# The last V block of each layer in smaller pieces, with more idle products, and one load without its padding: a two-layer decode step in fp32 on one core

## The chip, the core and the metric

The kernel runs on one core of one Trainium2 chip. The metric is the device time of one execution in microseconds (us). A time is given as the median of several executions; one further execution was profiled, and every duration below comes from that one.

## The reference

One token goes through two identical layers, each an attention block over a cache of 4096 positions and a two-matrix MLP, all in fp32:

```python
def _A_ref(x, k_cache, v_cache, wq, wo):          # x 1x1x512, caches 1x32x4096x128
    q = (x @ wq).reshape(1, 1, 32, 128).transpose(0, 2, 1, 3)
    scores = einsum("bhqd,bhkd->bhqk", q, k_cache) * 128 ** -0.5
    o = einsum("bhqk,bhkd->bhqd", softmax(scores), v_cache)
    return o.transpose(0, 2, 1, 3).reshape(1, 1, 4096) @ wo     # wo 4096x512
def _B_ref(x, w1, b1, w2, b2):                     # w1 512x1376, w2 1376x512
    return gelu(x @ w1 + b1) @ w2 + b2
x = A_x
for layer in range(2):                             # the same weights and caches twice
    x = x + _A_ref(layernorm(x), k_cache, v_cache, wq, wo)
    x = x + _B_ref(layernorm(x), w1, b1, w2, b2)
```

The caches are 67 MB each, so the data that two layers read is some 288 MB.

## The kernel before, in words

**Tiling.** The 32 heads are worked in 8 groups of 4. The K of a group, and its V, is a *block*: 128 partitions by 16384 fp32, 8 MiB. A block is 8 *chunks* of 2048 columns (`NC`), 1 MiB each; chunk c holds 512 positions of each of the 4 heads. The blocks and all weights pass through one large SBUF tile, `arena`, whose regions are reused in turn. Layer 0 takes the groups from 0 to 7, layer 1 from 7 to 0. So layer 1 starts on K and V blocks that are still in SBUF, and in its second group (`n == 1`) loads only what is missing of a block.

**One group.** The scores of a chunk (`scores`, L175) are 4 products into the PSUM bank `pS`; `softmax` reduces, exponentiates and transposes them (DVE L179 to L184, ACT L186, PE L188, then the copy `pt` L190); `values` (L201) multiplies each V chunk with its part of `pt`, 4 products that accumulate in `pO`. An fp32 product shows as two MATMUL records, so a chunk is 8 records of L175 or L201. `scaled_out` (L206 to L211) takes the wanted diagonal of `pO`, and `head_out` (L229) multiplies it with the group's `wo`, summed over the groups in `pB`.

**The last group of a layer** is cut finer. Its K comes in the pieces `LAST_K`, its V in those of `LAST`, one DMA for each, and PE waits for each piece apart. The first 7 chunks go the usual way; chunk 7 is done by `scaled_out_last` (L218, 32 short matmuls into a part of `pS`), so that the long transpose of the other chunks' result runs beside it. The two small operations L221 and L223 join both, and `head_out` reads `wo`, which comes in two halves. Then follow the layer norm and `mlp`: the `w1` products (L243), gelu on DVE and ACT, and the `w2` products (L262, 11 chunks of 8 records), whose weights come in the three pieces `W2_PARTS`.

**Idle products.** `idle(t, at)` (L287) is one product of the identity with a 512-column slice of the tile `t`, whose result nobody reads. It occupies PE for two records. After the last scores of a layer `FILL` of them write `pO`; one more stands behind some of the last V chunks and writes `pS`.

**The order of DMAs.** All large loads are issued by SP, in program order (`load`, L65). Each takes the next of eight completion semaphores, and SP waits, before it issues a load, until the load eight places earlier has landed and until the engines have finished with the region that it overwrites. The order at the end of a layer is: K of the last group, `w1` (layer 0 alone), V of the last group, the two halves of `wo`, the three pieces of `w2`. The first load of layer 1 (`wq`) overwrites the first chunks of `w2` in the region `SPARE`, so it waits for the L262 products that read them.

**Padding.** On the host, each HBM row of K, V and the weights gets 1024 unused columns behind it (`PITCH`), which sets the distance between rows. One load, in layer 1's second group, takes its source without an end: `v[g][:, n_kept:]`, with `n_kept` 9216.

Of the kernel before, what the change touches and what calls it, by code (L numbers as in the profile page):

```python
# [23 lines left out]
C = 8  # L24
# [5 lines left out]
NC = 4 * U  # L30
BLOCK = 8 * NC
# [6 lines left out]
PITCH = 1024  # L38
W2_PARTS = ((0, 6), (6, 9), (9, FB))
HIDDEN = ((0, 6), (6, FB))  # L40
FILL = 2
LAST = ((0, 4), (4, 5), (5, 6), (6, 7), (7, 8))
LAST_K = ((0, 4), (4, 6), (6, 7), (7, 8))
WHOLE, HALVES = ((0, 8),), ((0, 4), (4, 8))
VAR_AT = 1
# [3 lines left out]
def decode_layers(ctx: ExitStack, tc: tile.TileContext, x, k, v, w, w1, b1, w2, b2, out):  # L49
# [8 lines left out]
    def small(name, n=1):  # L58
        return work.tile([P, n], F32, name=name, bufs=2 if name in ("xs", "x_sum", "rstd", "sc", "nsc") else 1)
# [3 lines left out]
    def load(at, src):  # L63
        t = arena[:, at : at + src.shape[-1]]
        tc.keep_in_program_order(nc.sync.dma_start(t, src))  # L65
        return t
# [65 lines left out]
    def mean_of(xs, s, at):  # L132
        nm = minus_mean(s, at)
        xc, sq, ss = small("xc", 4), small("sq", 4), small("ss")
        nc.vector.tensor_scalar(xc, xs[:, :, 0], nm, None, op0=ALU.add)
        nc.vector.scalar_tensor_tensor(sq, xc, 1.0, xc, op0=ALU.mult, op1=ALU.mult, accum_out=ss)
        return nm, ss, xc

    def rstd_of(ss, at):
        nv = minus_mean(ss, at)  # L140
        ve, r = small("ve"), small("rstd")
        tc.keep_in_program_order(
            nc.vector.tensor_scalar(ve, nv, -1.0, EPS, op0=ALU.mult, op1=ALU.add))
        nc.gpsimd.tensor_tensor(r, ve, power, op=ALU.pow)
        return r

    def query_block(c, xs, wt):
        for j in range(J):
            nc.tensor.matmul(pQ[32 * j : 32 * j + 2, :], xs[:, c, :],  # L149
                             wt[:, c, :].rearrange("p (h j q) -> p j h q", h=4, j=J)[:, j],  # L150
                             start=(c == 0), stop=(c == 3))

    def first_queries(nm):
        qt = work.tile([P, P], F32, name="wide")
        nc.vector.transpose(qt, pQ)
        z = zq[0]
        nc.vector.scalar_tensor_tensor(z[:, :, C - 1], of_32(qt, J, 1), nm, of_32(qt, J),
                                       op0=ALU.mult, op1=ALU.add)
        return z
# [13 lines left out]
    def scores(z, c, kt):  # L173
        for j in range(J):
            nc.tensor.matmul(pS[32 * j : 32 * j + C, :], z[:, j, C - 1 - c : 2 * C - 1 - c],  # L175
                             kt[:, j, :], start=(c == 0), stop=(c == C - 1))
# [22 lines left out]
    def values(i, pt, vt, c, of=C):  # L199
        for j in range(J):  # L200
            nc.tensor.matmul(pO[32 * j : 32 * j + 4, :], pt[:, j, c, :], vt[:, j, :],  # L201
                             start=(i == 0), stop=(i == of - 1))
# [72 lines left out]
    def stream(what, g, pieces, base):  # L275

        for a, b in pieces:
            t = load(base + NC * a, part(k if what == "k" else v, g, a, b))
            for c in range(a, b):
                here[what, g, c] = chunk(t, c - a)  # L280
                yield c, here[what, g, c]
# [4 lines left out]
    def idle(t, at):  # L286
        tc.keep_in_program_order(nc.tensor.matmul(at[:C, :], ident[:, :C], t[:, 0, :], start=True, stop=True))  # L287

    for layer in range(2):
        order = list(range(G)) if layer == 0 else list(range(G))[::-1]  # L290
        for c in range(4):
            query_block(c, xs, wq_first)
            if c == 1:
                nm, ss, xc = mean_of(xs, s, pB[:, P : P + 1])
        negm, xc_l = small("negm"), small("xc_l", 4)
        nc.vector.tensor_copy(negm, nm)
        z = first_queries(negm)
        r = rstd_of(ss, pB[:, P + 1 : P + 2])
        nc.vector.tensor_copy(xc_l, xc)
        sc, nsc = small("sc"), small("nsc")  # L300
        nc.vector.tensor_scalar(sc, r, DH ** -0.5, None, op0=ALU.mult)
        nc.vector.tensor_scalar(nsc, r, -(DH ** -0.5), None, op0=ALU.mult)
        for n, g in enumerate(order):
            first, final = n == 0, n == G - 1

            k_home, v_home = ((2 * n + i) % 3 * BLOCK for i in (1, 2))
            if layer == 1:
                k_home, v_home = 12 * NC if n == 2 else BLOCK, 0

            if layer == 1 and n == 0:  # L310
                tiles = [(c, here["k", g, c]) for c in range(C)]
            elif layer == 1 and n == 1:
                tiles = [(c, here["k", g, c]) for c in range(2)]
                tiles += list(stream("k", g, ((2, 3), (3, 4), (4, 8)), -2 * NC))
            else:
                halves = first or (layer == 1 and n == 2)
                tiles = stream("k", g, LAST_K if final else HALVES if halves else WHOLE, k_home)
            for c, t in tiles:
                scores(z, c, t)
            if final:  # L320
                for _ in range(FILL):
                    idle(t, pO)
            pt, rl = softmax(sc, nsc)
            if layer == 1 and n == 0:
                z = queries(n + 1, xc_l, wq_next, pH, False)

            if layer == 1 and n == 0:
                for c in range(C):
                    values(c, pt, here["v", g, c], c)
            elif layer == 1 and n == 1:  # L330
                at, n_kept = 6 * NC, STAY + U * KEPT
                load(at + n_kept - 3 * NC, v[g][:, n_kept:])
                nc.scalar.copy(arena[:, at : at + STAY - 3 * NC], arena[:, SPARE - STAY + 3 * NC : SPARE])
                for i in range(KEPT):
                    to = at + STAY - 3 * NC + U * i
                    nc.scalar.copy(arena[:, to : to + U], pK[i])
                for c in range(C):
                    values(c, pt, here["v", g, c] if c < 3 else chunk(arena[:, at:], c - 3), c)
            elif final:
                if layer == 0:  # L340
                    load(HELD, w1)
                for c, t in stream("v", g, LAST, v_home):
                    if c < C - 1:
                        values(c, pt, t, c, C - 1)
                    if c == C - 2:
                        others = scaled_out(rl)
                    if 3 <= c < C - 1:
                        idle(t, pS)
            else:
                for c, t in stream("v", g, WHOLE, v_home):  # L350
                    for i in range(KEPT):
                        if layer == 0 and n == G - 2 and c == (STAY + U * i) // NC:
                            nc.scalar.copy(pK[i], t[:, STAY // U % J + i - J * (c - STAY // NC), :])
                    values(c, pt, t, c)

            if layer == 1 and n == 0:
                wo_t = chunk(arena[:, PAIR : PAIR + NC])
            elif final:
                last_v = t
                at = PAIR + NC * layer  # L360
                for i in range(2):
                    load(at + NC // 2 * i, of_w(wo_at(g), 1)[:, NC // 2 * i : NC // 2 * (i + 1)])
                wo_t = chunk(arena[:, at : at + NC])
                for a, b in W2_PARTS:
                    load(SPARE + U * a, w2[:, U * a : U * b])
            else:
                t = load(PAIR, of_w(wo_at(g) if layer == 0 else wq_at(g - 1), 2))
                wo_t, wq_next = (chunk(t, i) for i in ((0, 1) if layer == 0 else (1, 0)))
            on = scaled_out_last(rl, pt, last_v, others) if final else scaled_out(rl)
            head_out(on, wo_t, first, final)  # L370
            if not final and not (layer == 1 and n == 0):
                z = queries(n + 1, xc_l, wq_next, pO, layer == 0 and n == G - 2)
        at = work.tile([P, P], F32, name="wide")
        nc.vector.transpose(at, pW)
        x1, s1 = set_x(of_32(at, 4), 1.0, xs[:, :, 0])
        mt, xb = mlp(x1, s1, w1_t, w2_t)
        if layer == 0:
            xs, s = set_x(of_32(mt, 4), 0.5, xb)
            g = G - 2
            wq_first = wq_next  # L380
            wq_next = chunk(load(SPARE, of_w(wq_at(g), 1)))
            for c in range(2):
                here["k", g, c] = chunk(load(SPARE + NC * (c + 1), part(k, g, c, c + 1)))
# [43 lines left out]
```

## Time and profile before

| | |
|---|---|
| median of 3 executions | 685.1 us (684.95 to 686.89) |
| the profiled execution, its own time | 685.56 us |
| its span, first to last instruction | 683.8 us |
| mean granted TensorE clock | 0.748 |
| PE matmul busy | 362.6 us (53%) |
| VectorE busy | 111.8 us (16%) |
| ScalarE busy | 21.6 us (3%) |
| HBM read | 287.52 MB, 420 GB/s over the span |

The times of instructions and DMAs are counted from the start of the span. "PEclk" is the clock that TensorE was granted, 1.00 being full speed. The DMA share is the mean busy share of the core's 16 DMA engines; it can read a little over 1 in a short window.

### The profile page before, as it was taken

To read this page: it belongs to the slowest core of one execution; us is meant where nothing else is said; L and a number is where in the kernel's file an instruction comes from. 1 tells how busy PE (TensorE), PEld (TensorE's weight loads), DVE (VectorE), ACT (ScalarE), POOL (GpSimd) and SP (SyncE) were. 2 spreads that over 40 slices of the span, in tenths; PEclk is the share of its full clock that TensorE was granted. 3 is DMA by queue.
4 is the path that set the end of the run, shared out by engine and by line. 5 is a ranking of instruction groups with operands and counts; after the bars stand their busy time and mean duration, and the time that the engine had idled before them with its cause. 6 is when DMAs were issued, how large, how long until landed. Compare 5 with 4: busy or idle time off the path is not lost.

```text
span 683.8 us, 7178 instructions
## 1 busy us (share of the span) xinstructions
PE 362.6 (53%) x3240; PEld 106.2 (16%) x3240; DVE 111.8 (16%) x376; ACT 21.6 (3%) x48; POOL 3.5 (1%) x17
## 2 busy tenths in 40 slices
PE   2533563456534555246657886462345534655767
PEld 0001120011111111102114222110011111211213
DVE  1002120121201212012105122120121201202013
ACT  0000000000000000001000200000000000000000
POOL 0000000000000000000000000000000000000000
PEclk9967776766656777677769998676777757666889
DMA  9999999999999999999997999999999999999995
GB/s 369 430 433 453 453 427 429 426 430 427 429 427 422 450 441 434 429 406 428 440 407 320 442 425 452 437 427 429 429 430 427 434 430 414 453 434 414 428 411 217
DMA packets 11550, 287.97 MB, mean 421 GB/s; under 512 B 1792, under 2 KB 1792, under 8 KB 2816
## 3 DMA queue, kind: packets, MB, share of 16 engines
q1 hardware_dynamic: 11088, 287.51, 98.0%
q8 instruction: 25, 0.41, 0.2%
q10 hardware_dynamic: 432, 0.01, 0.0%
q14 instruction: 5, 0.04, 0.0%
HBM read 287.52 MB, written 0.00 MB: 420 GB/s over the span
## 4 chain that ended last, share of the span: by engine, by line
DMA 41%; PE 36%; another core or an unknown queue 16%; DVE 4%; ACT 1%; issue 1%; SPq 0%; ACTq 0%; DVEq 0%
DMA arena<-in_v 40%; PE pO L201 20%; PE pS L175 10%; PE pB L229 2%; ACT wide L186 1%; PE pS L287 1%; PE pO L168 1%; PE pO L188 1%; PE pO L262 1%; DMA xcol<-in_x 1%; DVE mx L179 1%; DVE wide L206 1%; PE pS L243 0%; PE pO L149 0%
## 5 line engine op out<-in xcount | busy, mean ns | idle before, releaser
L175 PE MATMUL pS<-arena,zq 128*8 128x512 f32 x1024 | 148.4, 730 | 136.5 <-DMA arena<-in_k 136.2
L201 PE MATMUL pO<-arena,pt 128*4 128x512 f32 x1008 | 148.0, 727 | 108.6 <-DMA arena<-in_v 108.2
L175 PEld LDWEIGHTS pS<-arena,zq 128*8 128x8 f32 x1024 | 29.7, 103 | 243.3 <-DMA arena<-in_k 137.5
L201 PEld LDWEIGHTS pO<-arena,pt 128*4 128x4 f32 x1008 | 28.8, 98 | 212.7 <-issue 211.4
L179 DVE TENSOR_REDUCE mx<-pS 128x1 f32<-128x512 f32 x16 | 11.1, 692 | 292.7 <-PE pS L175 292.7
L188 PE MATMUL pO<-ident,wide 128*128 128x128 f32 x64 | 12.3, 323 | 41.4 <-ACT wide L186 41.4
L186 ACT ACTIVATE wide<-pS,bias,sc 128x512 f32<-128x512 f32 x16 | 12.4, 777 | 548.8 <-DVE bias L184 548.8
L166 DVE SCALAR_TENSOR_TENSOR arena<-arena,xc_l 128x512 f32<-128x512 f32 x39 | 29.3, 752 | 1.4
L164 DVE TENSOR_SCALAR arena<-arena,xc_l 128x512 f32<-128x512 f32 x13 | 6.3, 486 | 130.9 <-DMA arena<-in_w 130.3
L206 DVE STREAM_TRANSPOSE wide<-pO 128x512 f32<-128x512 f32 x16 | 11.5, 717 | 89.7 <-PE pO L201 89.7
L229 PE MATMUL pB<-arena,on 128*1 128x128 f32 x448 | 18.6, 315 | 7.0 <-DVE on L211 7.0
L168 PE MATMUL pO<-one,arena 128*128 128x1 f32 x96 | 12.9, 256 | 11.0 <-DVE wide L206 9.3
L188 PEld LDWEIGHTS pO<-ident,wide 128*128 128x128 f32 x64 | 7.9, 159 | 55.4 <-ACT wide L186 50.4
L168 PEld LDWEIGHTS pO<-one,arena 128*128 128x128 f32 x96 | 11.9, 195 | 21.5 <-DVE wide L206 19.6
L229 PEld LDWEIGHTS pB<-arena,on 128*1 128x1 f32 x448 | 11.6, 93 | 12.1 <-DVE on L211 10.3
L287 PE MATMUL pS<-arena,ident 128*8 128x512 f32 x16 | 8.2, 592 | 0.0
L192 DVE STREAM_TRANSPOSE mt<-ls 128x32 f32<-128x32 f32 x16 | 3.4, 212 | 17.5 <-ACT wide L186 17.5
L262 PE MATMUL pO<-arena,gelu_g 128*1 128x128 f32 x176 | 5.2, 272 | 1.8 <-DVE gelu_g L258 1.8
L262 PEld LDWEIGHTS pO<-arena,gelu_g 128*1 128x1 f32 x176 | 4.3, 84 | 2.8 <-DVE gelu_g L258 2.5
L190 DVE COPY pt<-pO 128x128 f32<-128x128 f32 x16 | 4.2, 261 | 1.2 <-PE pO L188 1.2
L170 DVE COPY zq<-pO 128x4 f32<-128x4 f32 x13 | 2.1, 165 | 12.9 <-PE pO L168 12.9
L236 POOL TENSOR_TENSOR xb<-xs,b2c 128x4 f32<-128x4 f32 x2 | 0.4, 201 | 654.9 <-DVE xs L123 654.9
(94 smaller groups left out, 99.3 us busy)
## 6 DMA issues: line engine op xcount, KB each, us to landing
arena<-in_k SPq DMA_DIRECT2D x7, 4096.0 KB, 23.6
arena<-in_w SPq DMA_DIRECT2D x13, 2048.0 KB, 35.8
arena<-in_v SPq DMA_DIRECT2D x3, 4096.0 KB, 28.7
arena<-in_k SPq DMA_DIRECT2D x8, 1024.0 KB, 21.8
arena<-in_v SPq DMA_DIRECT2D x8, 1024.0 KB, 32.8
arena<-in_k SPq DMA_DIRECT2D x2, 2048.0 KB, 41.8
arena<-in_w SPq DMA_DIRECT2D x6, 512.0 KB, 25.2
arena<-in_w SPq DMA_DIRECT2D x2, 1536.0 KB, 25.9
```

Of the source, the lines that this page charges most:

```text
L164: nc.vector.tensor_scalar(t, wt[:, 0, :], xc[:, 0:1], None, op0=ALU.mult)
L166: nc.vector.scalar_tensor_tensor(t, wt[:, c, :], xc[:, c : c + 1], t, op0=ALU.mult, op1=ALU.add)
L168: nc.tensor.matmul(at[:, j : j + 1], t[:, P * j : P * (j + 1)], one, start=True, stop=True)
L175: nc.tensor.matmul(pS[32 * j : 32 * j + C, :], z[:, j, C - 1 - c : 2 * C - 1 - c], kt[:, j, :], start=(c == 0), stop=(c == C - 1))
L179: nc.vector.tensor_reduce(mx[:, 0:1], pS, axis=AX.X, op=ALU.max)
L186: nc.scalar.activation(p, pS, AF.Exp, bias=bias[:, 0:1], scale=sc, accum_out=ls[:, 0:1])
L188: nc.tensor.transpose(pT[:, b].rearrange("p j r -> p (j r)"), p[:, P * b : P * (b + 1)], ident)
L201: nc.tensor.matmul(pO[32 * j : 32 * j + 4, :], pt[:, j, c, :], vt[:, j, :], start=(i == 0), stop=(i == of - 1))
L206: nc.vector.transpose(ot[:, :512], pO)
L229: nc.tensor.matmul(pW[32 * j : 32 * j + 1, :], on[:, d : d + 1], wt[:, d, P * j : P * (j + 1)], start=first and d == 0, stop=final and d == 3)
L262: nc.tensor.matmul(pM[32 * j : 32 * j + 1, :], gs[c], w2_t[c][:, P * j : P * (j + 1)], start=(c == 0), stop=(c == FB - 1))
L287: tc.keep_in_program_order(nc.tensor.matmul(at[:C, :], ident[:, :C], t[:, 0, :], start=True, stop=True))
```

## The change

Three things are changed. The last V block of each layer is loaded as seven DMAs (chunks 0 and 1 together, then six single chunks) in place of five (chunks 0 to 3 together, then four single ones). One idle product now stands behind each of these pieces but the last (after chunks 1 to 6; it was after chunks 3 to 6), and three in place of two follow the last scores. And the one load that read the padding stops at the end of the block, so that it has 7168 columns in place of 8192.

```diff
-FILL = 2
-LAST = ((0, 4), (4, 5), (5, 6), (6, 7), (7, 8))
+FILL = 3
+LAST = ((0, 2), (2, 3), (3, 4), (4, 5), (5, 6), (6, 7), (7, 8))
...
                 at, n_kept = 6 * NC, STAY + U * KEPT
-                load(at + n_kept - 3 * NC, v[g][:, n_kept:])
+                load(at + n_kept - 3 * NC, v[g][:, n_kept:BLOCK])
...
                 for c, t in stream("v", g, LAST, v_home):
                     if c < C - 1:
                         values(c, pt, t, c, C - 1)
                     if c == C - 2:
                         others = scaled_out(rl)
-                    if 3 <= c < C - 1:
+                    if 0 < c < C - 1:
                         idle(t, pS)
```

In the rows that follow, "waits DMAHW3" is a wait for the completion semaphore number 3 of SP's loads, the sizes are partitions by columns of the result, and a minus or plus marks what stands there before or now. First PE in the last group of layer 0, from behind the last scores to the second V piece:

```order
-L287 MATMUL pO<-arena,ident 8x512 x2
+L287 MATMUL pO<-arena,ident 8x512 x3
 L188 MATMUL pO<-ident,wide 128x128 [waits Activation_49]
 L188 MATMUL pO<-ident,wide 128x128 x3
 L201 MATMUL pO<-arena,pt 4x512 [waits DMAHW7_49,DVE_49]
-L201 MATMUL pO<-arena,pt 4x512 x15
+L201 MATMUL pO<-arena,pt 4x512 x7
 L287 MATMUL pS<-arena,ident 8x512
 L201 MATMUL pO<-arena,pt 4x512 [waits DMAHW0_49]
```

PE's first wait for V is now for two chunks, and it has one more idle product ahead of the transposes L188. The same engine a little later, up to the short matmuls of chunk 7:

```order
 L201 MATMUL pO<-arena,pt 4x512 x3
 L287 MATMUL pS<-arena,ident 8x512
-L218 MATMUL pS<-arena,pt 1x128 [waits DMAHW3_49]
+L201 MATMUL pO<-arena,pt 4x512 [waits DMAHW3_49]
+L201 MATMUL pO<-arena,pt 4x512 x3
+L287 MATMUL pS<-arena,ident 8x512
+L201 MATMUL pO<-arena,pt 4x512 [waits DMAHW4_49]
+L201 MATMUL pO<-arena,pt 4x512 x3
+L287 MATMUL pS<-arena,ident 8x512
+L218 MATMUL pS<-arena,pt 1x128 [waits DMAHW5_49]
```

Two more chunks have a wait and an idle product of their own ahead of L218; the number of V products is the same. SP's queue at that place before, from `w1` over V and the two halves of `wo` to the first piece of `w2` (sizes are now partitions by columns loaded):

```order
L65 DMA arena<-in_w 128x5504 [waits DMAHW0_49,PE_49]
L65 DMA arena<-in_v 128x8192 [waits DMAHW7_49]
L65 DMA arena<-in_v 128x2048
L65 DMA arena<-in_v 128x2048 [waits DMAHW1_49]
L65 DMA arena<-in_v 128x2048 [waits DMAHW2_49]
L65 DMA arena<-in_v 128x2048 [waits DMAHW3_49]
L65 DMA arena<-in_w 128x1024 [waits DMAHW4_49,PE_49]
L65 DMA arena<-in_w 128x1024 [waits DMAHW5_49,PE_49]
L65 DMA arena<-in_w 128x3072 [waits DMAHW6_49,Activation_49]
```

And now:

```order
L65 DMA arena<-in_w 128x5504 [waits DMAHW0_49,PE_49]
L65 DMA arena<-in_v 128x4096 [waits DMAHW7_49]
L65 DMA arena<-in_v 128x2048
L65 DMA arena<-in_v 128x2048 [waits DMAHW1_49]
L65 DMA arena<-in_v 128x2048 [waits DMAHW2_49]
L65 DMA arena<-in_v 128x2048 [waits DMAHW3_49]
L65 DMA arena<-in_v 128x2048 [waits DMAHW4_49]
L65 DMA arena<-in_v 128x2048 [waits DMAHW5_49]
L65 DMA arena<-in_w 128x1024 [waits DMAHW6_49,PE_49]
L65 DMA arena<-in_w 128x1024 [waits DMAHW7_49,PE_49]
L65 DMA arena<-in_w 128x3072 [waits DMAHW0_49,Activation_49]
```

The four-chunk load has become a two-chunk load, two more single loads stand ahead of `wo`, and each load from there on is two semaphores further. The last group of layer 1 has the same pieces in the same order, without `w1`.

## The prediction

> **What bounds the kernel now.** First I read the page's row of DMA use, then the windows where it falls.
>
> ```profile
> DMA  9999999999999999999997999999999999999995
> ```
>
> ```profile
> 366.00:368.00 2.00, 1.36 (x41) 0.82 (x32) 1.39 (x6) 0.18 (x1) 0.62 (x2) 1.00 0.41 165
> 368.00:370.00 2.00, 1.72 (x64) 1.61 (x68) 1.07 (x7) 0.23 (x2) 0.00 (x0) 1.00 0.08 31
> 412.00:449.00 37.00, 17.15 (x124) 5.01 (x116) 6.56 (x19) 0.87 (x2) 0.00 (x0) 0.68 1.00 430
> 676.00:678.00 2.00, 1.44 (x44) 0.85 (x33) 1.31 (x6) 0.11 (x1) 0.55 (x1) 1.00 0.21 83
> ```
>
> A window row gives start:end, its length, the busy time of PE, PEld, DVE, ACT and POOL, the granted clock, the DMA share and GB/s. The DMA engines are full (share 1.00, 430 GB/s in layer 1) but for two places, the turn from layer 0 to layer 1 (366 to 370) and the end (from 676). There nothing is left to load until PE has come to the `w2` products (L262), and PE comes there along a chain that starts with the last V. So time can be won in two ways: fewer bytes, or an earlier end of that chain. The chain of work, in layer 0 and then in layer 1:
>
> ```profile
> 350.07 5.25 PE pO L201 x32
> ...
> 361.32 0.94 PE pS L218 x24
> 362.28 0.33 DVE wide L221
> ...
> 362.91 1.10 PE pB L229 x32
> ...
> 368.28 2.63 PE pO L262 x88
> ```
>
> ```profile
> 630.78 28.70 DMA arena<-in_v
> 659.62 5.78 PE pO L201 x32
> ...
> 668.82 0.43 PE pS L287
> 669.27 0.41 PE pS L287
> 669.68 0.86 PE pO L201 x5
> ...
> 671.39 0.94 PE pS L218 x24
> 672.36 0.33 DVE wide L221
> ...
> 672.99 1.10 PE pB L229 x32
> ...
> 678.36 2.63 PE pO L262 x88
> ```
>
> Columns: start, us, what. From its first V product (350.07 and 659.62) PE works without a wait up to L218: the four first chunks, then for each chunk a product of 0.86 and an idle product of 0.43 + 0.41. So L218 is late because PE is, if chunk 7 has landed by then. Issue times on SP, of `w1`, then for layer 0 and layer 1 each chunk 7, the second half of `wo` and the last piece of `w2` (both listed as in_w), and under them, in the same order, size and time from issue to landing:
>
> ```profile
> 317.88 0.33 SPq L65 DMA_DIRECT2D arena<-in_w  x1
> ...
> 328.70 0.33 SPq L65 DMA_DIRECT2D arena<-in_v  x1
> ...
> 333.71 0.33 SPq L65 DMA_DIRECT2D arena<-in_w  x1
> ...
> 352.44 0.33 SPq L65 DMA_DIRECT2D arena<-in_w  x1
> ...
> 638.92 0.33 SPq L65 DMA_DIRECT2D arena<-in_v  x1
> ...
> 647.32 0.33 SPq L65 DMA_DIRECT2D arena<-in_w  x1
> ...
> 661.98 0.33 SPq L65 DMA_DIRECT2D arena<-in_w  x1
> ```
>
> ```profile
> arena<-in_w SPq DMA_DIRECT2D x1, 2752.0 KB, 22.3
> ...
> arena<-in_v SPq DMA_DIRECT2D x1, 1024.0 KB, 31.2
> ...
> arena<-in_w SPq DMA_DIRECT2D x1, 512.0 KB, 28.7
> ...
> arena<-in_w SPq DMA_DIRECT2D x1, 512.0 KB, 16.8
> ...
> arena<-in_v SPq DMA_DIRECT2D x1, 1024.0 KB, 30.5
> ...
> arena<-in_w SPq DMA_DIRECT2D x1, 512.0 KB, 24.7
> ...
> arena<-in_w SPq DMA_DIRECT2D x1, 512.0 KB, 16.7
> ```
>
> Layer 0: `w1` lands at 340.18, chunk 7 at 359.90, `wo` whole at 362.41, `w2` whole at 369.24. Layer 1: chunk 7 at 669.42, `wo` 672.02, `w2` 678.68. Chunk 7 is there well over a microsecond before L218 is through the idle products ahead of it, above all in layer 1. This lateness, and the weights behind it, set the sum.
>
> **The change part by part.** *Two chunks first.* Between `w1` and chunk 7, layer 0 loads 4 MB as one piece by 349.93 (9.75 us; PE starts on it at 350.07, and in layer 1 a start stands 0.14 behind its landing, 630.78 + 28.70 against 659.62) and 4 MB as four pieces (9.97 us). The two first chunks then land at about 340.18 + 4.9 = 345.1, in layer 1 at about 654.7 (the same 4.9 ahead of 659.6). Work until the idle product of chunk 6 ends, at full clock: 7 x 0.86 + 6 x 0.85 = 11.1 us; until chunk 7 lands there are 14.8. Before, 32 products took 5.25 us in layer 0 where 3.44 would do, so the cold start costs some 1.8; with the two idle products that may fall into it still under 14. So PE catches up with the loads and L218 starts when chunk 7 lands. The three added idle products of each layer (two behind V, one behind the scores) cost nothing: the wait for V covers them, and if the cover went they would cost 0.85 each.
>
> *The third idle product behind the scores* must end before the transposes L188, or it delays softmax:
>
> ```profile
> 650.65 1.88 PE L287 MATMUL pO<-arena,ident 128*8 128x512 f32 x4
> ...
> 653.58 0.66 PE L188 MATMUL pO<-ident,wide 128*128 128x128 f32 x4 [1.05 <-ACT wide L186]
> 654.36 0.25 DVE L190 COPY pt<-pO 128x128 f32<-128x128 f32 x1
> ```
>
> Four records end at 652.53, six at about 653.4, 0.2 ahead of L188. Cost 0; at most 0.85, and that only in layer 1, where `pt` is ready at 654.61, just as V lands; in layer 0 there are 7 us between.
>
> *Two more DMAs a layer.* In layer 0 four pieces took 0.22 us more than one, 0.07 for each piece more. I take 0.15 for two, 0 to 0.4 as bounds, added to every later landing. On SP they stand ahead of `wo` and `w2`; the last `w2` piece waits for chunk 4 as before, 6 us ahead of its need. A rule speaks against this part. The Trainium skill (DMA: Bandwidth & Descriptors, Anatomy of one DMA) fits each DMA, on the GpSimd path, with a fixed 2.0 us besides its bytes. Four more would give 8 us if paid in series, and the sum below would turn to about 5 us slower; the pieces here are issued 30 us ahead, and the row above has 0.07.
>
> *Layer 0's chain.* L218 is 32 records of the shape of L229, which takes 1.10 for as many. So L218 runs from 359.90 + 0.15 + 0.14 = 360.19 to 361.29, and L221 starts 0.97 earlier than 362.28. That gain isn't kept: the second half of L229's records needs the second half of `wo`, there at 362.41 + 0.29 with the piece and the start, = 362.70. Half of L229 is 0.55 in; by the difference of 32 records in 1.10 and L218's 24 in 0.94, 16 take 0.32. I take 0.41 for the start of the second half, so it was 363.32. **Gain 0.62.** Next late would be the last `w2` piece: 369.24 + 0.29 = 369.53, its products due at 368.28 - 0.62 + 1.9 = 369.56 (72 of 88 records go ahead of them, 2.15 by their share of 2.63, less the length of one). It just fits, and the first load of layer 1 needs only the earlier ones:
>
> ```profile
> 369.39 0.33 SPq L65 DMA_DIRECT2D arena<-in_w  x1
> ```
>
> That load goes out 0.62 earlier. Since the DMA engines are empty there and full ever after, all of layer 1 moves with it.
>
> *The padding.* 1024 columns x 128 x 4 bytes = 0.52 MB, at 430 GB/s 1.22 us of full engines. **Gain 1.22**, between 0 (if something else held the stream) and 1.22. The shorter load also ends inside an earlier V chunk, so SP waits for one chunk less; the engines being full there, that is worth nothing.
>
> *Layer 1's chain.* L218 from 669.42 + 0.29 = 669.71 to 670.81, L221 1.53 earlier. The second half of `wo` at 672.02 + 0.29 = 672.31, against 672.99 + 0.41 = 673.40. **Gain 1.09.** The last `w2` piece is there at 678.97, due at 678.36 - 1.09 + 1.9 = 679.17: no new wait.
>
> Sum: 0.62 + 1.22 + 1.09 = 2.93 us. The profiled execution, 685.56 (span 683.8), would be 682.6 (680.9); it stands 0.46 above the median. From the median 685.1 that is **682.2 us**.
>
> **The rivals.** *1. PE goes cold in the pieces (slower).* It now waits some 0.75 us in each step of 2.49. At half clock a step takes 3.4, and PE falls behind.
>
> ```profile
> 648.00:650.00 2.00, 0.56 (x8) 0.12 (x8) 0.00 (x0) 0.00 (x0) 0.00 (x0) 1.00 1.11 475
> ...
> 656.00:658.00 2.00, 0.00 (x0) 0.00 (x0) 0.00 (x0) 0.00 (x0) 0.00 (x0) 0.80 0.91 381
> ```
>
> Against it: with PE busy for 0.56 of 2 us, in waits for K pieces, the clock stayed 1.00; it fell at about 657, after an idle stretch from 654.24. The Trainium skill (TensorE: Matmul & The Clock Gate, HAM oscillation) says the same, that idle gaps beyond some 3.4 us throttle the array; the trace agrees, with 2.8 to 3 us. Price: at half clock throughout, 22.2 us of work from 345.2, so L218 ends at 368.5 in place of 362.26, 6.2 later, and 678 for 672.3 in layer 1, 5.7 later: 685.1 + 11.9 - 1.2 = about 696. It turns the forecast into a loss below a mean clock of about 0.67 in the pieces (11.1 / 16.6).
>
> *2. The early start is not carried through layer 1*, because some wait of SP on PE there keeps its place. 0.62 is lost: 682.8. For it: many waits of SP are for PE. Against: share 1.00 for 37 us.
>
> *3. The pieces are dearer (no change).* At 0.5 us each, every landing is 1 us late in each layer instead of 0.15: layer 0 loses 0.23, layer 1 gains 0.24, the padding 1.22: 683.9. For it: the bytes of `wo` and `w2` land last of all, so any delay counts in full. Against: 0.07 by the row.
>
> *4. The padding was hidden*, for instance because the next loads of layer 1 wait for PE: 685.1 - 1.71 = 683.4.
>
> *5. A fixed cost per DMA in series (slower).* The nearest row is a load's smallest relative, the store of the result:
>
> ```profile
> out<-y SPq DMA_DIRECT2D x1, 2.0 KB, 1.4
> ```
>
> 4 x 1.4 = 5.6, against a gain of 3.23 without any piece cost: 687.5. It decides from 0.8 a piece. This is the page's rule of above, at the trace's price.
>
> **How the numbers follow.** Forecast 0.60, rival 1 0.04, 2 0.14, 3 0.14, 4 0.06, 5 0.02. Under 0.3% (2.05 us, about what can be told from no change here) is above 683.05: the forecast and 2 are faster, 0.74; 3 and 4 the same, 0.20; 1 and 5 slower, 0.06. Low end: no piece cost, and `wo` not the limit, so that the chains give 0.97 + 0.15 and 1.53 + 0.15: 685.1 - 4.0 = 681.1, rounded to 681.0. High end: rival 3, 684.0.
>
> **What the changed profile would show.** The first V product at about 345.2 in layer 0, and in layer 1 some 15 us ahead of L218; a wait for V ahead of each later chunk, at clock 1.00; L218 waiting for in_v and L229 for in_w; the first load of layer 1 at 368.8; HBM read 0.52 MB less; in layer 1 every landing 1.8 earlier; L262 there 7.7 behind the landing of chunk 7 (now 8.9). It is wrong if the clock falls between the pieces, if L188 starts later than 2.9 behind the last scores, if layer 1's landings move by less than 1.5, or if L262 waits for in_w.

## The result, and the profile after

| | before | after |
|---|---|---|
| median of 5 executions | 685.25 us (684.95 to 686.89) | 681.97 us (681.90 to 682.14) |
| the profiled execution, its own time | 685.56 us | 681.98 us |
| its span | 683.8 us | 680.1 us |
| mean granted TensorE clock | 0.748 | 0.752 |

The ratio of the times is 0.9947, with a 95% interval of 0.9932 to 0.9961: the change saves 3.3 us where 2.9 were forecast.

From the page of after, the row of DMA use over the span and the sum of the bytes, and then the two windows at the turn from layer 0 to layer 1 (start:end, length, busy time of PE, PEld, DVE, ACT and POOL, granted clock, DMA share, GB/s):

```profile
DMA  9999999999999999999998999999999999999996
...
HBM read 286.99 MB, written 0.00 MB: 422 GB/s over the span
```

```profile
366.00:368.00 2.00, 1.08 (x40) 0.67 (x32) 1.70 (x9) 0.21 (x1) 0.10 (x1) 1.00 0.47 184
368.00:370.00 2.00, 2.00 (x84) 1.80 (x72) 0.50 (x3) 0.21 (x1) 0.00 (x0) 1.00 0.38 90
```

The DMA engines are full but for the same two places as before, 0.53 MB less is read, and the hole at the turn has become smaller: from 368 to 370 the share is 0.38, where it was 0.08.

**Layer 0.** First PE in the last group, from the timeline of after (start, us, engine, line, what; in brackets the idle time ahead and what ended it), then the chain of work through `wo` at the same place:

```profile
337.48 0.66 PE L188 MATMUL pO<-ident,wide 128*128 128x128 f32 x4 [0.20 <-ACT wide L186]
...
345.22 3.59 PE L201 MATMUL pO<-arena,pt 128*4 128x512 f32 x16 [7.09 <-DMA arena<-in_v]
...
357.65 1.04 PE L201 MATMUL pO<-arena,pt 128*4 128x512 f32 x8 [0.70 <-DMA arena<-in_v]
...
360.19 1.05 PE L218 MATMUL pS<-arena,pt 128*1 128x128 f32 x32 [0.66 <-DMA arena<-in_v]
```

```profile
345.15 17.51 DMA arena<-in_w
362.70 0.66 PE pB L229 x16
...
367.63 2.63 PE pO L262 x88
```

PE starts on V at 345.22, with two chunks in place of four. By chunk 6 (357.65) it has caught up with the loads and waits for the piece, and L218 has an idle time of 0.66 us that ends with a landing, where before it had none. Then the second half of `wo` (345.15 + 17.51 = 362.66) releases the second half of L229, and L262 comes at 367.63 in place of 368.28.

**Layer 1.** The same places, and SP's issue of chunk 7 with its size and the time to landing:

```profile
652.07 1.90 PE L201 MATMUL pO<-arena,pt 128*4 128x512 f32 x16 [0.54 <-DVE rl L196]
...
659.45 1.04 PE L201 MATMUL pO<-arena,pt 128*4 128x512 f32 x8 [0.62 <-DMA arena<-in_v]
...
666.92 1.05 PE L218 MATMUL pS<-arena,pt 128*1 128x128 f32 x32 [0.63 <-DMA arena<-in_v]
...
669.45 0.62 PE L229 MATMUL pB<-arena,on_all 128*1 128x128 f32 x16 [0.16 <-DMA arena<-in_w]
```

```profile
644.62 0.33 SPq L65 DMA_DIRECT2D arena<-in_v  x1
```

```profile
arena<-in_v SPq DMA_DIRECT2D x1, 1024.0 KB, 22.3
```

Chunk 7 lands at 644.62 + 22.3 = 666.9, and L218 starts with it; before, it landed at 669.42 and 24 of its 32 records came at 671.39 or later. Again L229 waits for `wo`. In layer 0 PE starts on V at half clock. Later the clock holds in the waits, as windows of after show, two of layer 0 and one of layer 1:

```profile
345.00:348.00 3.00, 2.78 (x16) 0.57 (x17) 0.00 (x0) 0.00 (x0) 0.00 (x0) 0.50 1.00 418
...
357.00:360.00 3.00, 1.88 (x10) 0.29 (x10) 1.12 (x3) 0.00 (x0) 0.00 (x0) 1.00 1.03 421
...
658.00:661.00 3.00, 2.38 (x12) 0.29 (x10) 0.00 (x0) 0.00 (x0) 0.00 (x0) 1.00 1.02 426
```

**Between them.** The load that lost its padding (`in_v`, 3584 KB), with the K load that lands ahead of it: issue times, and under them sizes and times to landing, first of after, then of before:

```profile
378.16 0.33 SPq L65 DMA_DIRECT2D arena<-in_k  x1
388.83 0.33 SPq L65 DMA_DIRECT2D arena<-in_v  x1
```

```profile
arena<-in_k SPq DMA_DIRECT2D x1, 4096.0 KB, 16.3
arena<-in_v SPq DMA_DIRECT2D x1, 3584.0 KB, 14.1
```

```profile
378.80 0.33 SPq L65 DMA_DIRECT2D arena<-in_k  x1
390.29 0.33 SPq L65 DMA_DIRECT2D arena<-in_v  x1
```

```profile
arena<-in_k SPq DMA_DIRECT2D x1, 4096.0 KB, 16.1
arena<-in_v SPq DMA_DIRECT2D x1, 4096.0 KB, 15.4
```

Now V lands 402.93 - 394.46 = 8.5 us behind K; before, 405.69 - 394.90 = 10.8. That is 2.3 us less for bytes worth 1.22. The first experiments ask why.

The account of the two profiled executions: 0.65 us from layer 0 (368.28 to 367.63); 2.1 more by the last K of layer 1 (it lands 2.7 earlier); 1.26 more by L262 (678.36 to 674.38, 3.98 in all). The stretch from the store of the result to the end of the span is 0.28 longer than before, which leaves the spans' difference of 3.7. That stretch took 2.23 to 2.25 us in the four kept traces with as many loads as before and 2.52 in the seven with as many as after, so it comes with the change; why, no run shows.

The 2.1 us are not the padding alone. Of the 0.65, the issue of layer 1's first load shows 0.64, its landing 0.57, and the landing of the K load behind it 0.45 (377.64 and 377.19). The V load adds the 2.3. After it, the step to one landing is 1.39 us late in after (at 583.78) and another 1.18 late in before (at 644.93), which all but cancel.

### The profile page after: what moved, and what is told of

It reads as the page before. It is cut to its first block, busy times and chain, and to the rows that moved or that the text cites. A ratio compares the mean times of both kernels' runs of the same rounds, so it can differ in the third digit from the quotient of the medians.

```text
span 680.1 us, 7208 instructions
## 1 busy us (share of the span) xinstructions
PE 372.0 (55%) x3252; PEld 107.2 (16%) x3252; DVE 112.1 (16%) x376; ACT 21.7 (3%) x48; POOL 3.6 (1%) x17
## 4 chain that ended last, share of the span: by engine, by line
DMA 44%; PE 33%; another core or an unknown queue 16%; DVE 4%; ACT 1%; issue 1%; SPq 0%; ACTq 0%; DVEq 0%
DMA arena<-in_v 39%; PE pO L201 18%; PE pS L175 10%; DMA arena<-in_w 5%; PE pB L229 1%; ACT wide L186 1%; PE pO L168 1%; PE pO L188 1%; PE pO L262 1%; DMA xcol<-in_x 1%; DVE mx L179 1%; DVE wide L206 1%; PE pS L243 0%; PE pO L149 0%
## 5 line engine op out<-in xcount | busy, mean ns | idle before, releaser
L175 PE MATMUL pS<-arena,zq 128*8 128x512 f32 x1024 | 151.7, 745 | 133.4 <-DMA arena<-in_k 132.6
L201 PE MATMUL pO<-arena,pt 128*4 128x512 f32 x1008 | 145.8, 722 | 98.5 <-DMA arena<-in_v 97.5
L188 PE MATMUL pO<-ident,wide 128*128 128x128 f32 x64 | 13.7, 351 | 39.7 <-ACT wide L186 39.7
L229 PE MATMUL pB<-arena,on 128*1 128x128 f32 x448 | 17.6, 304 | 7.0 <-DVE on L211 7.0
L188 PEld LDWEIGHTS pO<-ident,wide 128*128 128x128 f32 x64 | 8.8, 174 | 53.7 <-ACT wide L186 48.7
L168 PEld LDWEIGHTS pO<-one,arena 128*128 128x128 f32 x96 | 11.9, 194 | 21.5 <-DVE wide L206 19.6
L229 PEld LDWEIGHTS pB<-arena,on 128*1 128x1 f32 x448 | 11.2, 90 | 11.8 <-DVE on L211 10.3
L287 PE MATMUL pS<-arena,ident 128*8 128x512 f32 x24 | 12.6, 608 | 0.0
L262 PE MATMUL pO<-arena,gelu_g 128*1 128x128 f32 x176 | 5.2, 272 | 1.8 <-DVE gelu_g L258 1.8
L287 PE MATMUL pO<-arena,ident 128*8 128x512 f32 x12 | 5.5, 592 | 0.0
L262 PEld LDWEIGHTS pO<-arena,gelu_g 128*1 128x1 f32 x176 | 4.3, 83 | 2.8 <-DVE gelu_g L258 2.5
```

The lines of the kernel that those rows point to most:

```text
L168: nc.tensor.matmul(at[:, j : j + 1], t[:, P * j : P * (j + 1)], one, start=True, stop=True)
L188: nc.tensor.transpose(pT[:, b].rearrange("p j r -> p (j r)"), p[:, P * b : P * (b + 1)], ident)
L229: nc.tensor.matmul(pW[32 * j : 32 * j + 1, :], on[:, d : d + 1], wt[:, d, P * j : P * (j + 1)], start=first and d == 0, stop=final and d == 3)
L262: nc.tensor.matmul(pM[32 * j : 32 * j + 1, :], gs[c], w2_t[c][:, P * j : P * (j + 1)], start=(c == 0), stop=(c == FB - 1))
```

## The experiments

Medians, the range of the executions, and the ratio to the kernel before on the same chip with its 95% interval. The kernel before had medians of 685.2, 685.41 and 685.61 in the three series.

| run | median us | range | ratio |
|---|---|---|---|
| e1 padding alone | 683.88 | 682.3 to 684.91 | 0.9979 [0.9971, 0.9988] |
| e2 pieces and idle products alone | 683.3 | 683.14 to 686.22 | 0.9978 [0.9968, 0.9988] |
| e3 idle products as before | 682.62 | 682.5 to 682.69 | 0.9962 [0.995, 0.9974] |
| e4 no idle products | 685.31 | 681.9 to 687.97 | 0.9993 [0.9978, 1.0009] |
| e5 half of the last `wo` | 681.18 | 680.99 to 681.52 | 0.9938 [0.9925, 0.995] |
| e6 `wo` in four loads | 681.85 | 681.52 to 681.95 | 0.9946 [0.9933, 0.9958] |
| e7 code moved | 683.11 | 682.22 to 683.68 | 0.9964 [0.9951, 0.9978] |
| e8 eight single chunks | 682.03 | 681.63 to 682.25 | 0.9948 [0.9936, 0.9961] |
| e9 e3 with its code moved | 682.25 | 681.86 to 682.36 | 0.995 [0.9937, 0.9962] |
| e10 four-chunk piece, all idle products | 687.49 | 686.89 to 688.66 | 1.0033 [1.002, 1.0045] |
| e11 four-chunk piece, one idle product | 681.43 | 681.36 to 681.84 | 0.9941 [0.9929, 0.9954] |
| e12 the changed kernel again | 682.21 | 682.03 to 682.33 | 0.995 [0.9937, 0.9964] |

The theory was the prediction's: PE's lateness at chunk 7, and 1.22 us of bytes. The diffs below are against the changed kernel, except that of e1.

### e1 and e2: the two parts apart

e1 is the kernel before with `v[g][:, n_kept:BLOCK]`. e2 is the changed kernel without it:

```diff
-                load(at + n_kept - 3 * NC, v[g][:, n_kept:BLOCK])
+                load(at + n_kept - 3 * NC, v[g][:, n_kept:])
```

> The kernel before with the shorter load alone. Both theories agree that it is faster; they differ in how much. Theory A (bytes): 0.52 MB at 430 GB/s, 1.22 us, so 684.0 against 685.25; the load lands 9.8 us behind the K piece ahead of it (10.76 before), still with the 1 us that the code fetch of 16 KB at 400 us adds on one DMA engine. Theory B (the padded read itself is dear): the whole 2.2 us by which that step shortened between the two profiles, 683.0, the load 8.5 us behind the K piece.

> The changed kernel, but the one load reads its padding again: the pieces and the idle products alone. Theory A: 0.6 in layer 0 and 1.1 to 1.4 in layer 1, so 1.7 to 2.0 faster than before, 683.3 to 683.5; the padded load some 9.7 us behind the K piece if no code fetch falls on the engine that is last, 10.8 if one does. Theory B: 1.1 to 1.2 faster, 684.1, the padded load 10.8 us behind the K piece in any case.

They saved 685.2 - 683.88 = 1.3 us and 685.2 - 683.3 = 1.9 us, together 3.2 of the whole change's 3.3: the parts add up. In e2, which still reads the padding, the issues of the same K and V load, with their times to landing:

```profile
378.80 0.33 SPq L65 DMA_DIRECT2D arena<-in_k  x1
390.29 0.33 SPq L65 DMA_DIRECT2D arena<-in_v  x1
```

```profile
arena<-in_k SPq DMA_DIRECT2D x1, 4096.0 KB, 15.9
arena<-in_v SPq DMA_DIRECT2D x1, 4096.0 KB, 14.1
```

V is 404.4 - 394.7 = 9.7 us behind K. In e1, without the padding, the step is 8.5, as in after. So the padding is worth 9.7 - 8.5 = 1.2 us, its bytes. The 8.5 was the sign that e1's expectation gave to a dear padding, but e2 speaks against it: it reads the padding without the other microsecond of before's 10.8. In before, the last of the 16 DMA engines' completions for this load came 2.75 us behind the first, against 1.91 in after. One execution of before was profiled, so whether each has this late step isn't shown.

### e3, e9 and e4: the idle products

e3 puts the idle products back as they were; e9 is e3 with six matmuls of one column added in layer 0's second group, far from the places in question; e4 has no idle product at all (`FILL = 0`, none behind V).

```diff
-FILL = 3
+FILL = 2
...
-                    if 0 < c < C - 1:
+                    if 3 <= c < C - 1:
```

> The changed kernel with the idle products of before (two behind the last scores, one behind each of chunks 3 to 6): what do the added three a layer do? My theory: nothing, they lie in waits for V, and the clock holds without them: 682.0, within 0.2. Rival: without them PE is slower to reach full clock in layer 0 and is late at chunk 7: 0.5 to 2 us slower than the changed kernel, with a clock under 1.00 between 351 and 358.

> e3_old_idles with six one-column products added in layer 0's second group, where PE waits for V: the same number of PE instructions as the changed kernel has, so its code blocks end at the same places in the tail, but still the old idle products. In e3_old_idles PE stood still for 0.64 us in the middle of the w1 products of layer 1 with nothing to wait for, 1.7 us behind a code fetch. Theory C (the added idle products matter only by moving the code): that stop is gone, 682.0, as the changed kernel on the same chip within 0.15. Rival (they matter by what they do to PE or its clock): as e3_old_idles, 682.6.

> The changed kernel without any idle product behind the last scores or the V pieces. PE is then busy for 0.86 of each 2.49 us. Theory 1 (a third of the time is enough, as between the K pieces, where the clock stayed 1.00 at 28%): 682.0, within 0.3. Theory 2 (the clock falls or never rises): chunk products of 1.7 still fit into 2.49, but L218 and what follows up to the w2 products run at half clock, 1 us more in L218 and 2 to 3 in the rest, in each layer: 685 to 689, PEclk 0.50 after 350.

e3 was slower than the changed kernel by 0.6 us, where 0.2 was the most that was expected, but not where the idle products stand: in layer 1 chunk 7 and `wo` land as in after (666.85 and 669.40). The loss is later, in the `w1` products. L243 in the timelines of e3 and then of e9:

```profile
672.24 1.20 PE L243 MATMUL pB<-arena,xs 128*2 128x152 f32 x28
674.08 0.43 PE L243 MATMUL pB<-arena,xs 128*2 128x152 f32 x4 [0.64 <-issue]
```

```profile
672.62 1.22 PE L243 MATMUL pB<-arena,xs 128*2 128x152 f32 x32
```

In e3, PE stops for 0.64 us between two equal products, with no wait that the profile shows ("issue"). In e9 the stop is gone, and the time is 682.25, against 682.21 for the changed kernel itself on the same chip. So the added idle products are worth nothing at the place where they stand; leaving them out cost e3 its 0.6 us by the stop, which came and went with the position of the code. The trace has a fetch of instructions that started at 671.7 in e3, in e9 one at 668.4. That PE waited for its next block of code is a guess: the fetch in e3 had ended at 672.7, ahead of the stop at 673.44, and in e11 a fetch at 671.5 goes without a stop.

e4 scattered over 6 us. Its profiled execution (682.28 us) is one of the fastest of 12, and already shows the clock falling in layer 1, in V products with the idle time ahead of them and in two windows of 2 us:

```profile
659.85 1.04 PE L201 MATMUL pO<-arena,pt 128*4 128x512 f32 x8 [1.45 <-DMA arena<-in_v]
662.34 1.89 PE L201 MATMUL pO<-arena,pt 128*4 128x512 f32 x8 [1.44 <-DMA arena<-in_v]
```

```profile
661.00:663.00 2.00, 0.66 (x4) 0.11 (x8) 0.00 (x0) 0.00 (x0) 0.00 (x0) 0.84 0.98 410
663.00:665.00 2.00, 1.41 (x12) 0.11 (x8) 0.00 (x0) 0.00 (x0) 0.00 (x0) 0.50 1.00 412
```

Without idle products the waits grow to 1.45 us, and the granted clock falls to 0.84 and 0.50 between the pieces; the same 8 records then take 1.89 us in place of 1.04. A wait of this length alone doesn't do it, for layer 0 of the same execution has such waits at full clock:

```profile
355.59 1.04 PE L201 MATMUL pO<-arena,pt 128*4 128x512 f32 x8 [1.44 <-DMA arena<-in_v]
358.08 1.04 PE L201 MATMUL pO<-arena,pt 128*4 128x512 f32 x8 [1.45 <-DMA arena<-in_v]
```

```profile
357.00:360.00 3.00, 1.04 (x8) 0.11 (x8) 0.78 (x2) 0.00 (x0) 0.00 (x0) 1.00 1.03 416
```

In all 14 traces the granted clock changes in steps of 3.41 us. In the step ahead of the fall at 662.35 PE was busy for 1.05 us, 31%; in the steps of layer 0 from 351.73 to 361.97 it was busy for 44% or more. No trace holds 1.00 behind a step with less than 41%, though the clock also fell behind steps with more, up to 71%. The earlier idle products (after chunks 3 to 6) are enough to prevent the fall here; none is not. That the slower executions are those in which the clock fell more, or earlier, is likely, but none of them was profiled, and their mean clocks fit it only loosely (0.724 at 687.97 us, but 0.741 at 686.75).

### e5 and e6: is the second half of `wo` the limit?

e5 doesn't load the second half of the last group's `wo` and uses the first half twice; e6 loads `wo` in four parts.

```diff
-                                  wt[:, d, P * j : P * (j + 1)],
+                                  wt[:, d % 2 if final else d, P * j : P * (j + 1)],
...
-                for i in range(2):
+                for i in range(1):
```

> The changed kernel without the load of the second half of wo in the last group of each layer; head_out takes the first half twice there. If wo is what holds L229, as I worked out, L229 now follows L223 without a wait: 0.35 sooner in layer 0, 0.4 in layer 1, so 0.75 faster than the changed kernel, 681.2. If something else held the chain (chunk 7, DVE, or w2), the same time within 0.2. The loads saved are worth nothing by themselves, as the engines run empty behind them.

> The changed kernel with the wo of the last group in four loads in place of two, so that three quarters of L229 can go ahead of the last landing. By the same theory the part behind the landing shrinks from 16 records (0.66) to 8 (0.45), 0.2 a layer, less two pieces more at 0.07 to 0.12: 0 to 0.15 faster, 681.8. A rival by which pieces are nearly free: 0.4 faster, 681.6; by which short rows are dear: 0.5 slower.

L229 in layer 1 of e5, one unbroken row where after has two with a wait for in_w between:

```profile
668.72 1.05 PE L229 MATMUL pB<-arena,on_all 128*1 128x128 f32 x32 [0.70 <-DVE on_all L223]
```

With 681.18, e5 is 0.8 us faster over the two layers: this is what the wait for `wo` costs now, with the bytes that e5 spares. The profiles agree: from the landing of `w1` to the first load of layer 1, e5 took 0.46 us less than after, and from that of the last K to the store of the result 0.36 less. Four loads in place of two (681.85) changed nothing that can be told from the 681.97 of after.

### e8: the price of a piece

```diff
-LAST = ((0, 2), (2, 3), (3, 4), (4, 5), (5, 6), (6, 7), (7, 8))
+LAST = ((0, 1), (1, 2), (2, 3), (3, 4), (4, 5), (5, 6), (6, 7), (7, 8))
```

> The changed kernel with the first V piece split as well, eight single chunks: one load and one wait more a layer. My theory: a piece costs 0.07 to 0.12 of landing and PE gains nothing, since it waits for chunk 7 anyway: 0.1 to 0.2 slower than the changed kernel, 682.1 to 682.2. Rival: a dear piece, 0.5 each: 683.0. An earlier start of the clock would be worth nothing.

Measured 682.03, which can't be told from the 681.97 of after. From the landing of `w1` to that of chunk 7, layer 0 took 19.70 us with five pieces (before), 19.96 with seven, 20.06 with eight; layer 1, from the last K, 19.67, 19.85 and 19.89. Over all kept traces, the four with five pieces took 19.65 to 19.70 in either layer and the nine with seven 19.80 to 20.07, so a piece costs 0.05 to 0.2 us.

### e7: does code alone move the time?

```diff
+            if layer == 0 and n in (1, 2):
+                for _ in range(16):
+                    tc.keep_in_program_order(
+                        nc.tensor.matmul(pO[:C, :1], ident[:, :C], t[:, 0, :1], start=True, stop=True))
```

> The changed kernel with 32 tiny products (one column) added in layer 0's second and third group, where PE waits for V anyway: about half a 16 KB block of PE's code more, so all later code fetches come earlier in the program. Theory A: a fetch delays one DMA engine by about 1.2 us, and the stream only if that engine is the last one; so the time moves by up to 1.2 us either way (680.8 to 683.2) though no path is touched, and in the profile the landing steps over 4.9 per 2 MB stand elsewhere. Rival: the fetches don't matter: 682.0 within 0.2, the same long steps.

These 32 one-column products stand where PE waits for loads, and the kernel became 1.1 us slower than after (the executions of the two don't overlap). Most loads of 8 MB take the 19.35 us of after, but three of e7 in layer 1 took 19.69, 19.75 and 20.00 (landing at 471.92, 535.27 and 603.75); one late step of after, 6.27 us for 2 MB up to 583.78, took 4.89 in e7. So some steps of the stream are late by up to 1.4 us, and which ones they are changes with the position of instructions in the program; in e12, the code of after executed once more, the two that are over 1 us late land where they do in after (at 309 and 584). The late microsecond of before's V load is a step of this size, too; it is not part of what the padding is worth.

### e10 and e11: is the smaller first piece needed?

The rival: what counts is that PE isn't late, whether by an earlier start or by fewer idle products. e10 keeps the changed kernel but for the four-chunk piece of before; e11 also has only the idle product behind chunk 6.

```diff
-LAST = ((0, 2), (2, 3), (3, 4), (4, 5), (5, 6), (6, 7), (7, 8))
+LAST = ((0, 4), (4, 5), (5, 6), (6, 7), (7, 8))
...
-                    if 0 < c < C - 1:
+                    if c == C - 2:
```

> The changed kernel with the V pieces of before (chunks 0 to 3 as one) but all the new idle products, so also those behind chunks 1 and 2. If PE's lateness behind that big piece is what the smaller one cured, the two added idle products now lie on the chain at 0.85 each: L218 2.9 to 3.3 us later than in the changed kernel, the whole 2 x 3.0 later, 688. If the pieces were not the cause: as the changed kernel, 682.

> The changed kernel with the V pieces of before, but only one idle product behind them, after chunk 6. By the same theory the idle products of before, 0.85 each with no wait to cover them, made PE late, not the size of the first piece as such: without three of them PE is through chunk 6 and its idle product 0.7 us ahead of chunk 7, which lands 0.15 to 0.2 sooner as there are two pieces fewer. Then the time is that of the changed kernel or up to 0.4 less, 681.6 to 682.0. It is more if the clock falls in the waits, as in e4_no_idles (up to 685).

> The changed kernel itself, for the three others on this chip. 682.0, within 0.2.

e10, layer 0: the first V products and L218, and under them the same and layer 1's L218 in e11.

```profile
350.22 3.60 PE L201 MATMUL pO<-arena,pt 128*4 128x512 f32 x16 [11.90 <-DMA arena<-in_v]
...
363.14 1.04 PE L218 MATMUL pS<-arena,pt 128*1 128x128 f32 x26
```

```profile
350.18 7.03 PE L201 MATMUL pO<-arena,pt 128*4 128x512 f32 x48 [11.92 <-DMA arena<-in_v]
...
360.03 1.05 PE L218 MATMUL pS<-arena,pt 128*1 128x128 f32 x32 [0.62 <-DMA arena<-in_v]
...
666.61 1.05 PE L218 MATMUL pS<-arena,pt 128*1 128x128 f32 x32 [0.61 <-DMA arena<-in_v]
```

With the late start and all idle products, L218 has no idle time ahead of it and ends at 364.18, where after has 361.24: 687.49, slower than before. With the same late start and one idle product a layer behind V, PE catches up, waits 0.6 us for chunk 7 in both layers, and the kernel takes 681.43 us, 0.8 less than the changed kernel on the same chip and a little less than the 681.6 to 682.0 expected. So the smaller first piece isn't needed. What made PE late before were idle products that no wait covered: the start on V came late, and those behind chunks 3 to 6 were paid in full. e11 is the fastest complete version, with as many DMAs as before and fewer idle products. The spans of e11 and e12 differ by 0.78 us. Of that, 0.50 stands ahead of the store of the result; the four pieces that e11 doesn't load account for it (0.39 in layer 0 and 0.17 in layer 1, by the landings as in e8). The other 0.28 is the stretch behind the store, as long as in before.

## Why the prediction was right, point by point

- **The sum.** 682.2 was forecast, with 2.93 us saved; 681.97 came, with 3.3. The signs, places and causes of all three terms hold. By the measured sizes below, the terms make 3.1, and less the 0.28 behind the store, which the sum left out, 2.8. The 0.5 up to 3.3 belongs to no term; the late steps of the stream are of that size. So that the number came so close is in part luck.
- **Layer 0's chain: 0.62, measured 0.65.** L218 at 360.19 as worked out to the hundredth (by two errors that cancel, see below), the second half of L229 at 362.70, the first load of layer 1 at 368.75 (forecast 368.8).
- **The padding: 1.22, measured 1.2** (e1 against e2). The check named for it, every landing of layer 1 earlier by 1.8, read 0.45 ahead of the V load, 2.7 behind it, 1.27 at 583.78 (under the 1.5 named as a sign of being wrong) and 2.7 again at the last K, with the late steps told above. A check of this size in one pair of executions can't be read to better than a microsecond here.
- **Layer 1's chain: 1.09, measured 1.26** (against the last K of the layer). This term was under-sized: the second half of L229 began 0.05 us behind the landing of `wo`, not the assumed 0.14. The 0.14 was read behind idle times of 11.9 and 5.4 us; behind waits of less than 1.5 us at full clock it was 0.04 to 0.05 in all 14 traces. And `wo` was whole 2.52 us behind chunk 7 (666.88 and 669.40) in place of the 2.60 of before. L262 came 7.5 behind chunk 7's landing, forecast 7.7.
- **Two more DMAs: 0.15 a layer, measured 0.26 and 0.18.** Somewhat dearer, within the bounds; in layer 0 this and the 0.05 of above cancel.
- **Idle products at no cost where a wait covers them, 0.85 each where none does.** Both held. The third behind the scores ended 0.20 us ahead of L188, as worked out. The wait for V ahead of each later chunk, named as a sign, came in layer 1 from chunk 3 on; in layer 0, where PE ran at half clock until 349.4, only from chunk 6 on, and there the waits for chunks 6 and 7 (0.70 and 0.66 us) cover the two added behind V. The price is seen in e10, which has two uncovered idle products a layer more than before: before's 685.61 less e1's 1.3 for the padding is 684.3, and e10 is 3.2 above it, where four at 0.85 make 3.4.
- **What the prediction didn't see:** that the early start was only one of two ways to take the lateness away. Its own rows showed it, idle products of 0.84 us in a chain where nothing was waited for.
- **The rivals.** *1, a cold PE:* behind the cold start of layer 0 the clock stayed at 1.00 in the pieces, but this rival was nearer than its 0.04 says, as e4 shows: without idle products the clock fell among waits of 1.45 us, not the 2.8 to 3 read from the trace of before. The Trainium skill (TensorE: Matmul & The Clock Gate, HAM oscillation) has idle gaps above some 3.4 us as the danger; e4's windows show the clock falling with gaps less than half as long, when PE was busy for a third of the time, so here the measurement decides. The 2.8 to 3 us that the prediction took for agreement lie below that figure, too. And the stretch that spoke against this rival, PE busy for 0.56 of 2 us from 648 to 650, lies in a step of the clock (646.96 to 650.37) in which PE was busy for 1.63 of 3.41 us, 48%. *2, the early start lost:* the first load of layer 1 went out 0.64 us earlier and landed 0.57 earlier; the K loads behind it show 0.45, so in this pair some 0.2 of the start was lost. *3 and 5, dear pieces:* 0.05 to 0.2 us each, not 0.5 or 1.4. *4, a hidden padding:* e1 alone saves 1.3.

## What to carry to other kernels

Look in the chain for filler work that runs without a wait ahead of it: filler that keeps the clock up is free only in front of a wait, and each piece of it elsewhere delays the end. When the last products of a stream start late, count whether they can catch up without the filler before the stream is cut finer, since finer pieces cost something too. And where two kernels differ by a microsecond in one pair of profiles, run one with nothing but its code moved before that microsecond is given a cause.

## What the hardware did that was not expected

Instruction fetches. The queue table of after has them in a row of its own (packets, MB, share of 16 engines):

```profile
q8 instruction: 25, 0.41, 0.2%
```

That is 25 blocks of 16 KB, 0.2% of the DMA time, and yet code that had only been moved changed the time by 1.1 us (e7), and a stop of PE of 0.64 us came and went with the position of code (e3 and e9). The Trainium skill (Runtime: NRT & Kernel Launch, Instruction fetch mechanics) describes blocks of 16 KiB that the sequencer fetches on its own queue while it executes, at a cost that is mostly hidden. The row agrees in size; "mostly" is where these runs differ, for in a kernel whose DMA engines are full a fetch shares them with the loads. That the fetches have a part in the late steps, a count over the 14 traces shows (loads of 2 MB and more that landed from 60 to 645 us, without the turn from 340.5 to 396; a step runs from one landing to the next). There 28 steps were late by 1.03 to 1.55 us, and a fetch started inside each of them; of the 322 steps without a fetch, none was late by more than 0.4. A fetch alone isn't enough: 223 steps had one and were less than 0.9 late. In before's V load a fetch started at 400.2 and one DMA engine came late, while in after one at 398.8 and in e2 one at 400.1 fell into the same load and cost nothing. What decides between them stays open.
